# A fused routing-attention and expert kernel: the second pair's keys turned on TensorE in the prologue

## The chip, the cores and the metric

The kernel runs on one core of a Trainium2 chip. The metric is the device time of one execution in microseconds. Three runs of the kernel before gave 945.76, 945.78 and 945.89 us; the median is 945.78. A core has TensorE (PE in the profile; its weight loads are PEld), VectorE (DVE), ScalarE (ACT), GpSimd (POOL) and the DMA queues, of which that of SyncE (SP) issues nearly all loads here.

## The reference

Two blocks are computed one after the other. The first is attention in which a query may look only at keys that were assigned to the same one of 16 centroids:

```
q_assign = argmax(q_n . c_n)          # 4 batches, 8 heads, 768 tokens, 64 values a head
k_assign = argmax(k_n . c_n)          # q_n, k_n, c_n: divided by their lengths
mask     = q_assign[:, None] == k_assign[None, :]
scores   = where(mask, scale * q @ k.T, -1e9)
attn     = softmax(scores, over the keys)
x        = attn @ v
```

The second is `h = x @ w_in`, `g = h * erf(softplus(h))`, `out = g @ w_out` with 3072 tokens, 512 inputs and 2048 inner values. All inputs and the output are float32.

## The kernel before

The 32 combinations of batch and head are worked as 16 pairs of heads. For a pair, `qT` and `kT` hold queries and keys with the 2 x 64 values of the heads on the 128 partitions and the 768 tokens in a row. The function `load` brings queries and keys in by 32 x 32 blocks: four DMAs a tensor, each for one head and half its values, so that one VectorE transpose by blocks of 32 (`transposes`, or `transposed_part` for some columns) makes `qT` or `kT`. Values `v` are loaded token by token in two DMAs. Pair 1's queries and keys use `x_more` as their place, since the ordinary buffers hold pair 0.

For each pair, `similarities` makes the products with the centroids into PSUM bank `turned[1]`, and `choose`, a generator, goes on in steps on VectorE: `sims` (a transpose), a maximum over the centroids, `hot` (which centroid is the maximum), `hotT` (its transpose). It stops behind each step until the code calls `next` or `run`. `masks` multiplies `hotT` by a constant matrix `pick` and copies the product into `qm` or `km`, the rows that add a large number where query and key were assigned alike. `vectors` makes the bfloat16 copies `qv` and `kv`.

`maxima_step` finds the greatest score of each query ahead of the exponentials: a pass of `qv` with `kv` and a pass of `qm` with `km` add up in PSUM (`wide`, or in the prologue `also`, two banks each), and VectorE reduces them into `nmx`. When half of a pair's queries are done, VectorE reduces `nmx` into `lowest`, and `turn` puts the results into a row of `qm` by TensorE and ScalarE. Then come, for each half of the queries and each block of 128 keys (a unit), `products` (scores into `sc`), `scores` (the masks added to them), `curve` (the exponential on ScalarE), `accumulate` (GpSimd) and `attend` (products with `v` into `turned[0]` or `turned[1]`).

The order is written out by hand. Every instruction keeps its program order on its engine. Waits between engines follow from the tiles that instructions read and write.

The prologue runs from the loads to the loop over `period`. It makes pair 0's `qT`, `kT`, similarities, `choose(0)`, three of the four masks, then the five maxima steps of `FIRST_STEPS`, alternating between `also` and `wide`, then `step_ahead(0, 0)`, the next such step, then `turn(0, 0)` and the transposes of pair 1. Between these lie `warm` calls, products on TensorE whose results nobody reads. In `period(0, 0)` the code issues `products`, `step_ahead(0, 1)`, `scores`, `curve`, and then the similarities of pair 1; `period(0, 1)` begins with `step_ahead(0, 2)`, which writes `wide` again. The rest of `choose(1)` is spread over these two periods.

`places` are five staging areas for the weights of the second block; the fifth is a part of `x_more`, and `fetch` of it stands behind the prologue's last transposes on SP's queue.

Of the kernel before, what the change touches and what calls it, by code (L numbers as in the profile page):

```python
# [139 lines left out]
def kernel(  # L140
# [84 lines left out]
    def load(p, nm, src, pl):  # L225
        if p >= NPAIR:
            return
        b, h0 = heads(p)
        if nm == "v":
            t = pl.tile([P, NJ, 2, D], F32, name="in_v")  # L230
            for e in range(2):
                queues[0].dma_start(out=t[:, :, e], in_=src[b, h0 + e].rearrange("(j p) d -> p j d", p=P))
        else:

            if pl is None:
                t = x_more.rearrange("p a k t -> p (a k t)")[:, (nm == "k") * S : (1 + (nm == "k")) * S]
                t = t.rearrange("p (n t) -> p n t", t=Q)
            else:
                t = pl.tile([P, NB, Q], F32, name="in_" + nm)
            for e in range(2):  # L240
                for g in range(D // Q):
                    queues[e if nm == "q" else e * g].dma_start(
                        out=t[e * D + g * Q : e * D + (g + 1) * Q],
                        in_=src[b, h0 + e, :, g * Q : (g + 1) * Q].rearrange("(n t) d -> t n d", t=Q),
                    )
        pairs.setdefault(p, {})[nm] = t
# [143 lines left out]
    def transposed_part(p, nm, lo, hi):  # L390

        st = pairs[p]
        t = st[nm].rearrange("p n t -> p (n t)")
        ve.transpose(out=rows[p % 3][nm][:, lo:hi], in_=t[:, lo:hi])
        if hi == S:
            st[nm + "T"] = rows[p % 3][nm]
            del st[nm]

    def similarities(p, groups=range(4), lo=0, hi=HW):

        if p >= NPAIR:
            return
        st = pairs[p]
        st["psim"] = turned[1][:, 0:HW]
        for g in groups:
            te.matmul(
                st["psim"][2 * C * g : 2 * C * (g + 1), lo:hi], lhsT=ccT[:, p % HP],
                rhs=st["qk"[g // 2] + "T"][:, g % 2 * HW + lo : g % 2 * HW + hi],
                start=True, stop=True,
            )  # L410

    def choose(p, spare=None, aside=False):

        if p >= NPAIR:
            return
        st = pairs[p]
        n = HW // C
        sims = routep.tile([P, HW], F32, name="sims")
        ve.transpose(out=sims, in_=st.pop("psim"))
        yield  # L420
        sim = sims.rearrange("p (g c) -> p g c", c=C)
        mx = (wide[:, 0] if spare is None else spare)[:, 512 - n :]
        ve.reduce_max(out=mx, in_=sim, axis=AX.X)
        yield
        hot = routep.tile([P, HW], BF16, name="hot")
        ve.tensor_tensor(
            out=hot.rearrange("p (g c) -> p g c", c=C), in0=sim,
            in1=mx.unsqueeze(2).to_broadcast([P, n, C]), op=ALU.is_equal,
        )
        yield  # L430
        if aside:
            st["aside"] = routep.tile([P, HW], BF16, name="aside")
            ve.transpose(out=st["aside"][D + Q :], in_=hot[D : D + Q])
            yield
        st["hotT"] = routep.tile([P, HW], BF16, name="hotT")
        ve.transpose(out=st["hotT"], in_=hot)
# [978 lines left out]
    def period(p, i):  # L1415
        u = 2 * NJ * p + 2 * i
        n1, n2 = 2 * p - 1, 2 * p
        early = lambda n: 0 <= n < N_EARLY

        def mask(place):  # L1420
            which = (MASKS if p else FIRST_MASKS).get((i, place))
            if which:
                return masks(p + 1, *which, turned[0 if i in (0, 5) else 1], place == 2)
            return lambda: None

        if u > 0:
            for which in turns if i in (0, 3) else ():
                turn(*which)
                turns.remove(which)
            if i == 3 and not p:  # L1430
                transposes(2, "k")
            if i == 3 and p:
                similarities(p + 2)
                routing[0] = choose(p + 2, turned[0], True)
            step_ahead(p, 2 * i)
            if i == 3 and p:
                next(routing[0], None)
            if i == 2:
                transposes(p + 2, "k" if p else "q")
        mask(0)()  # L1440
        if i == 0 and early(n1 - 1):
            sign(n1 - 1)
        elif i == 3 and early(n1):
            sign(n1)
        if i == 4:
            next(routing[0], None)
        next(part[0], None)
        if i == 0 and p:
            run(routing[0])
            transposes(p + 2, "q")  # L1450
        if u == 2:
            next(routing[0])
            next(routing[0])
        products(u)
        mask(3)()
        products(u + 1)
        mask(1)()
        second = step_ahead(p, 2 * i + 1, True) if u > 0 else iter(())
        next(second, None)
        if u == 0:  # L1460
            step_ahead(0, 1)
        rows = D if u == 0 or u + NJ + 2 >= len(units) else Q
        scores(u, rows)
        next(second, None)
        next(second, None)
        next(part[0], None)
        if i == 5:
            next(routing[0], None)
        scores(u + 1, rows)
        later = mask(2)  # L1470
        if i == 3 and not p:
            similarities(p + 2)
            routing[0] = choose(p + 2, turned[0], True)
        if i == 0:
            later()
            curve(u)
        else:
            curve(u)
            later()
        curve(u + 1)  # L1480
        if u == 0:
            similarities(1)
            routing[0] = choose(1, turned[1])
            next(routing[0])
            vectors(1, "q")
            vectors(1, "k")
        if i == 0 and early(n1 - 1):
            bounded(n1 - 1)
            shifted(n1 - 1)
        elif i == 1 and early(n1):  # L1490
            size_and_rest(n1)
        elif i == 5 and early(n2):
            rest(n2)
        for _ in range(FORMS.get(p, {}).get(i, 0)):
            x_forms.pop(0)() if x_forms else forms.pop(0)[0]()
        if i == 3:
            if not p:
                next(routing[0], None)
            if early(n1):
                bounded(n1)  # L1500
                shifted(n1)
        elif i == 1:
            load(p + 1, "v", v, vp)
            if p == 0:
                run(routing[0])
        elif i == 4:
            vectors(p + 2, "k")
            vectors(p + 2, "q")
        if u > 0:
            if i == 1 and early(n1 - 1):  # L1510
                summed(n1 - 1)
            elif i == 4 and early(n1):
                summed(n1)
            if i in POOL_FORMS.get(p, ()) and forms:
                forms.pop(0)[1]()
            for w in (u - 2, u - 1):
                accumulate(w)
            for w in (u - 2, u - 1):
                attend(w)
            if i == 3:  # L1520
                next(routing[0], None)
            if i % HJ == 0 and u - 1 != LATE or u - 3 == LATE:
                part[0] = divide(u - 1 - u % NJ)
                next(part[0])
        if i == 3 and early(n2):
            size(n2)
# [29 lines left out]
    for r in (0, D):  # L1556
# [8 lines left out]
    products(0)  # L1565
    warm(9, turned[0], zeros)
    run(choose(0))
    copies = [
        masks(0, nm, half, bank)
        for nm, half, bank in (("q", 0, wide[:, 0]), ("k", 0, turned[0]), ("k", 1, turned[1]))  # L1570
    ]
    transposed_part(1, "q", 0, 2 * P)
    ve.tensor_scalar_max(out=st["qm"][:, 0:HW], in0=wide[:, 0, 0:HW], scalar1=0.0)
    transposed_part(1, "q", 2 * P, 5 * P)
    for copy in copies[1:]:
        copy()
    load(0, "v", v, vp)
    for n in range(len(places) - 1):
        fetch(n)
    for i, pieces in enumerate(FIRST_STEPS):  # L1580
        run(maxima_step(0, pieces, wide if i % 2 else also, by_products=True))
        if i == 1:
            masks(0, "q", 1, turned[1])()
        if 0 < i < len(FIRST_STEPS) - 1:
            warm(2, turned[0], zeros)
    step_ahead(0, 0)
    warm(2, turned[0], zeros)
    turn(0, 0)
    transposed_part(1, "q", 5 * P, S)
    turns.clear()  # L1590
    transposes(1, "k")
    fetch(len(places) - 1)
    queues[0] = queues[1] = sy
    for p in range(NPAIR):
# [108 lines left out]
```

## Time and profile before

| what | value |
|---|---|
| profiled execution | 945.83 us |
| its span | 944.1 us |
| PE busy | 938.0 us (99%) |
| DVE busy | 784.3 us (83%) |
| ACT busy | 546.6 us (58%) |
| POOL busy | 506.4 us (54%) |
| TensorE clock granted, first 10 us | 1.00 |

The times in the rows below are microseconds from the start of the span; a row of a timeline gives the start, the length, the engine, the line, the operation, the tiles `out<-in`, the shape and the count, and in brackets how long the engine sat idle before and who ended that. All instructions that a helper records have one line, L131, so the tile names tell them apart; `sc` in the prologue is `also` as well as the score tiles, since they share a pool. A row of the chain is start, length and what set the pace. In a group of instructions the numbers behind the bar are the busy time in us and the mean ns of one. In a table of windows each engine's busy time and count stand in the order PE, PEld, DVE, ACT, POOL, and then the clock granted to TensorE, the share of the DMA engines and GB/s.

### The profile page before, as it was taken

Reading aid. Unit: us, or ns where it says so; the run is one execution under the profiler, and the core shown is the slowest. Engines: PE = TensorE matmul, PEld = TensorE weight load, DVE = VectorE, ACT = ScalarE, POOL = GpSimd, SP = SyncE. Lnnn points to the kernel's source line nnn. Section 1 sums busy time; section 2 is a strip of 40 time slices with the busy share of each in tenths; the row PEclk is TensorE's granted clock in tenths of the full one; section 3 lists DMA queues with packets and bytes.
Section 4 is the critical chain, followed back from the end, with each engine's and each line's share of the span. In section 5 each row is a group of like instructions: output and inputs, shape, how many; then the busy total and the mean of one; then the engine's idle time right before and its main releaser. Section 6 shows DMA issues by size and latency. Waiting matters only on the chain.

```text
span 944.1 us, 22367 instructions
## 1 busy us (share of the span) xinstructions
PE 938.0 (99%) x8775; PEld 708.9 (75%) x8775; DVE 784.3 (83%) x1416; ACT 546.6 (58%) x809; POOL 506.4 (54%) x365
## 2 busy tenths in 40 slices
PE   8999999999999999999999999999999999999998
PEld 4555555555555555688888889998999899989987
DVE  8888888888888887879886688689868977897887
ACT  4777777777777776476413553663257236525541
POOL 2688888888888888999119111450063016103600
PEclk9999999999999999999999999999999999999999
DMA  9345545554443621133875257353453436343433
GB/s 215 79 112 113 113 113 114 113 114 112 113 112 68 156 56 38 24 128 127 219 249 219 83 125 221 106 175 118 151 176 128 136 120 202 118 150 123 157 112 111
DMA packets 176352, 123.17 MB, mean 130 GB/s; under 512 B 132600, under 2 KB 143352, under 8 KB 176248
## 3 DMA queue, kind: packets, MB, share of 16 engines
q1 hardware_dynamic: 171880, 116.34, 43.2%
q0 software_dynamic: 1872, 4.98, 2.9%
q8 instruction: 69, 1.13, 0.5%
q10 hardware_dynamic: 2496, 0.43, 0.2%
q14 instruction: 35, 0.29, 0.1%
HBM read 91.78 MB, written 23.33 MB: 122 GB/s over the span
## 4 chain that ended last, share of the span: by engine, by line
PE 98%; DVE 1%; SPq 0%; DMA 0%; issue 0%; DVEq 0%
PE bank L131 43%; PE turned L131 32%; PE sc L131 17%; PE wide L131 6%; DVE nmx L131 1%; SPq L131 0%; DMA qm<-least_rows 0%; DVE sims L131 0%; DVE hotT L131 0%; DVE wide L131 0%; DVE hot L131 0%; DVE qm L131 0%; DVE qT L131 0%; DVE osb L131 0%; DVEq L1698 0%
## 5 line engine op out<-in xcount | busy, mean ns | idle before, releaser
L131 POOL TENSOR_TENSOR more_out<-more_out,pr 128x768 f32<-128x768 f32 x128 | 217.1, 1696 | 15.4 <-ACT pr L131 5.4
L131 DVE TENSOR_REDUCE nmx<-wide 128x2 f32<-128x512 f32 (+4 forms) x189 | 179.4, 950 | 45.6 <-PE wide L131 44.5
L131 ACT ACTIVATE pr<-sc 128x768 f32<-128x768 f32 x192 | 148.4, 810 | 80.4 <-PE wide L131 73.8
L131 PE MATMUL turned<-pr,in_v 128*32 128x193 f32 x3072 | 145.2, 330 | 0.0
L131 POOL TENSOR_TENSOR g<-g 128x512 f32<-128x512 f32 x36 | 47.1, 1308 | 180.8 <-DVE g L131 178.9
L131 PEld LDWEIGHTS turned<-pr,in_v 128*32 128x32 f32 x3072 | 90.2, 109 | 51.0 <-issue 27.0
L131 DVE TENSOR_TENSOR g<-g 128x512 f32<-128x512 f32 x132 | 90.8, 688 | 23.2 <-PE bank L131 12.2
L131 PE MATMUL sc<-qT,kT 64*128 64x384 f32 x528 | 98.7, 485 | 0.0
L131 DVE TENSOR_TENSOR g<-bank,g 128x256 f32<-128x256 f32 (+1 forms) x128 | 64.6, 531 | 18.2 <-PE bank L131 9.5
L131 PE MATMUL bank<-g_more,g 128*128 128x256 f32 (+1 forms) x328 | 75.7, 374 | 0.0
L131 PE MATMUL bank<-x_own,w_in 128*128 128x128 f32 (+1 forms) x440 | 74.0, 310 | 0.0
L131 ACT ACTIVATE a_s<-g 128x1024 f32<-128x1024 f32 x38 | 39.6, 1055 | 57.5 <-POOL g L131 44.7
L131 POOL TENSOR_TENSOR more_out<-pr,pr 128x768 f32<-128x768 f32 x32 | 59.6, 1861 | 14.9 <-ACT pr L131 14.9
L131 PEld LDWEIGHTS bank<-g_more,g 128*128 128x128 f32 x328 | 61.2, 190 | 8.1
L131 PEld LDWEIGHTS bank<-x_own,w_in 128*128 128x128 f32 x440 | 63.2, 191 | 4.4 <-issue 0.6
L131 DVE TENSOR_TENSOR g<-a_s,g 128x512 f32<-128x512 f32 x76 | 66.2, 892 | 0.4 <-ACT a_s L131 0.4
L131 PE MATMUL wide<-kv,qv 64*128 64x512 bf16 (+4 forms) x380 | 64.4, 326 | 0.5 <-DVE nmx L131 0.5
L131 PE MATMUL bank<-w_out,g 128*128 128x256 f32 x280 | 64.5, 379 | 0.0
L131 PE MATMUL wide<-km,qm 32*128 32x512 bf16 (+5 forms) x380 | 62.0, 325 | 0.0
L131 ACT ACT_TABLE_LOAD x40 | 51.3, 1283 | 17.9 <-DVE g L131 17.3
L131 PEld LDWEIGHTS <-qv 64*128 64x128 bf16 x386 | 23.0, 93 | 51.4 <-issue 37.1
L131 PEld LDWEIGHTS sc<-qT,kT 64*128 64x128 f32 x528 | 46.3, 187 | 18.6 <-issue 1.3
(245 smaller groups left out, 1992.6 us busy)
## 6 DMA issues: line engine op xcount, KB each, us to landing
g_more<-b_dram SPq DMA_DIRECT2D x52, 512.0 KB
g_more<-w_dram SPq DMA_DIRECT2D x84, 256.0 KB
x_own<-in_moe_w_in_dram SPq DMA_DIRECT2D x13, 512.0 KB
in_v<-in_v_dram SPq DMA_DIRECT2D x32, 192.0 KB
x_dram<-more_out SPq DMA_DIRECT2D x128, 48.0 KB
x_own<-x_dram SPq DMA_DIRECT2D x6, 1024.0 KB
in_k<-in_k_dram SPq DMA_DIRECT2D x59, 96.0 KB
in_q<-in_q_dram SPq DMA_DIRECT2D x58, 96.0 KB
```

The lines of the kernel that those rows point to most:

```text
L131: ins = getattr(self.engine, name)(*args, **kw)
```

## The change

Pair 1's keys are loaded token by token, with two DMAs like those of the values, into the same part of `x_more`. Six float32 transposes on TensorE (`turned_by_products`), three behind the second maxima step into `turned[0]` and three behind the third into `turned[1]`, with one ScalarE copy of 384 columns each, make `kT`; the VectorE transpose of the keys and two of the `warm` calls go. Pair 1's queries are turned in two VectorE pieces and not three, both ahead of the maxima.

The similarities of pair 1 stand before `step_ahead(0, 0)`, and the first two steps of `choose(1)` behind it; `hot` moves to `period(0, 0)` and `hotT` to the start of `period(0, 1)`.

The product for the first half of pair 0's query mask is made in two parts: 128 columns into `wide`, copied by VectorE, and 256 columns into `also[:, 0, 256:512]`, copied by ScalarE behind the two key masks.

```diff
@@ load
-        if nm == "v":
-            t = pl.tile([P, NJ, 2, D], F32, name="in_v")
+        if nm == "v" or (nm == "k" and pl is None):
+            if nm == "v":
+                t = pl.tile([P, NJ, 2, D], F32, name="in_v")
+            else:
+                t = x_more.rearrange("p a k t -> p (a k t)")[:, S : 2 * S]
+                t = t.rearrange("p (j e d) -> p j e d", j=NJ, e=2)
             for e in range(2):
                 queues[0].dma_start(out=t[:, :, e], in_=src[b, h0 + e].rearrange("(j p) d -> p j d", p=P))
...
+    def turned_by_products(p, nm, bank, half):
+
+        st = pairs[p]
+        st[nm + "T"] = rows[p % 3][nm]
+        for j in range(HJ):
+            te.transpose(
+                out=bank[:, j * P : (j + 1) * P],
+                in_=st[nm][:, half * HJ + j].rearrange("p e d -> p (e d)"), identity=ident,
+            )
+        ae.copy(out=st[nm + "T"][:, half * HW : (half + 1) * HW], in_=bank[:, 0:HW])
...
@@ period
         if u == 2:
-            next(routing[0])
-            next(routing[0])
+            run(routing[0])
...
         if u == 0:
-            similarities(1)
-            routing[0] = choose(1, turned[1])
             next(routing[0])
             vectors(1, "q")
             vectors(1, "k")
...
         elif i == 1:
             load(p + 1, "v", v, vp)
-            if p == 0:
-                run(routing[0])
...
@@ prologue
-    copies = [
-        masks(0, nm, half, bank)
-        for nm, half, bank in (("q", 0, wide[:, 0]), ("k", 0, turned[0]), ("k", 1, turned[1]))
-    ]
+    first_queries, other_queries = wide[:, 0, 0:P], also[:, 0, 2 * P : 2 * P + HW - P]
+    te.matmul(first_queries, lhsT=pick[0:D, 0], rhs=st["hotT"][0:D, 0:P], start=True, stop=True)
+    te.matmul(other_queries, lhsT=pick[0:D, 0], rhs=st["hotT"][0:D, P:], start=True, stop=True)
+    copies = [masks(0, "k", half, turned[half]) for half in range(2)]
     transposed_part(1, "q", 0, 2 * P)
-    ve.tensor_scalar_max(out=st["qm"][:, 0:HW], in0=wide[:, 0, 0:HW], scalar1=0.0)
-    transposed_part(1, "q", 2 * P, 5 * P)
-    for copy in copies[1:]:
+    ve.tensor_scalar_max(out=st["qm"][:, 0:P], in0=first_queries, scalar1=0.0)
+    transposed_part(1, "q", 2 * P, S)
+    for copy in copies:
         copy()
+    ae.activation(out=st["qm"][:, P:HW], in_=other_queries, func=ACT.Relu)
...
-        if 0 < i < len(FIRST_STEPS) - 1:
+        if i in (1, 2):
+            turned_by_products(1, "k", turned[i - 1], i - 1)
+        elif i == 3:
             warm(2, turned[0], zeros)
+    pairs[1].update(lows[1])
+    del pairs[1]["k"]
+    similarities(1)
     step_ahead(0, 0)
+    routing[0] = choose(1, turned[1])
+    next(routing[0])
+    next(routing[0])
     warm(2, turned[0], zeros)
     turn(0, 0)
-    transposed_part(1, "q", 5 * P, S)
     turns.clear()
-    transposes(1, "k")
```

More of the change, by code (lines that the diff above doesn't have):

```diff
@@ L235, in load @@
             if pl is None:
-                t = x_more.rearrange("p a k t -> p (a k t)")[:, (nm == "k") * S : (1 + (nm == "k")) * S]
+                t = x_more.rearrange("p a k t -> p (a k t)")[:, 0:S]
                 t = t.rearrange("p (n t) -> p n t", t=Q)
```

## The prediction

> **What bounds the kernel now.** I read the page first, then the chain that ended last in order of time, then the start of each engine's timeline, and last the waits and the loads. The page's rows of span, busy time and chain:
>
> ```profile
> span 944.1 us, 22367 instructions
> PE 938.0 (99%) x8775; PEld 708.9 (75%) x8775; DVE 784.3 (83%) x1416; ACT 546.6 (58%) x809; POOL 506.4 (54%) x365
> PE 98%; DVE 1%; SPq 0%; DMA 0%; issue 0%; DVEq 0%
> ```
>
> TensorE carries 98% of the chain, so a shift of TensorE's start of steady work travels to the end one to one, unless a later wait absorbs it. The change lies wholly before the main loop and in its first two periods, so only the first 25 us matter. The chain there:
>
> ```profile
> 10.86 0.32 PE wide L131
> ...
> 11.23 0.55 DVE qm L131
> ...
> 12.26 5.17 DVE nmx L131 x5
> ...
> 17.53 0.19 DVE lowest L131
> ...
> 17.77 0.34 PE turned L131 x6
> ...
> 19.65 0.89 PE turned L131 x8
> ...
> 20.54 0.40 PE wide L131 x4
> 20.94 1.29 PE sc L131 x8
> ```
>
> To be seen: from 11.23 to 17.72 the end is set by VectorE (a mask, a transpose, five maxima, the `lowest` reduction), and from 17.77 on by TensorE alone, where the chain stays for the rest of the stretch. So two moments count: L, when `lowest` starts (17.53), and X, when `step_ahead(0, 2)` starts on TensorE (20.54). Whatever moves X moves the end. VectorE's own rows:
>
> ```profile
> 8.42 0.58 DVE L131 STREAM_TRANSPOSE sims<-turned 128x384 f32<-128x384 f32 x1 [0.62 <-PE turned L131]
> 9.04 0.56 DVE L131 TENSOR_REDUCE wide<-sims 128x24 f32<-128x384 f32 x1
> 9.64 0.55 DVE L131 TENSOR_TENSOR hot<-sims,wide 128x384 bf16<-128x384 f32 x1
> ...
> 10.73 0.40 DVE L131 STREAM_TRANSPOSE qT<-x_more 128x256 f32<-128x256 f32 x1
> 11.21 0.56 DVE L131 TENSOR_SCALAR qm<-wide 128x384 bf16<-128x384 f32 x1
> 11.69 0.57 DVE L131 STREAM_TRANSPOSE qT<-x_more 128x384 f32<-128x384 f32 x1
> 12.20 0.69 DVE L131 TENSOR_REDUCE nmx<-sc 128x2 f32<-128x512 f32 x1
> 12.81 1.22 DVE L131 TENSOR_REDUCE nmx<-wide 128x2 f32<-128x1024 f32 x1
> ...
> 17.62 0.95 DVE L131 TENSOR_REDUCE nmx<-wide 128x2 f32<-128x768 f32 x1
> 18.48 0.30 DVE L131 STREAM_TRANSPOSE qT<-x_more 128x128 f32<-128x128 f32 x1
> 18.71 0.93 DVE L131 STREAM_TRANSPOSE kT<-x_more 128x768 f32<-128x768 f32 x1
> 19.57 0.92 DVE L131 TENSOR_REDUCE nmx<-wide 128x2 f32<-128x768 f32 x1
> ```
>
> X follows the last of these: 19.57 + 0.92 = 20.49, and 0.05 later TensorE may overwrite `wide`. The similarities of pair 1 end at 19.65 + 0.89 = 20.54 too, so X is held twice over; taking one holder away frees nothing.
>
> **The change part by part.**
>
> *The first maxima step: where the new wait is.* Rows of TensorE and ScalarE at that place, and ScalarE's group for a 256-column read of PSUM:
>
> ```profile
> 11.88 0.28 PE L131 MATMUL sc<-km,qm 64*128 64x256 bf16 x2 [0.41 <-ACT km L131]
> 11.99 0.39 PE L131 MATMUL wide<-kv,qv 64*128 64x512 bf16 x2
> ...
> 12.82 0.50 PE L131 MATMUL turned<-lowest,identb 128*128 128x384 bf16 x2
> 13.25 0.39 PE L131 MATMUL sc<-kv,qv 64*128 64x512 bf16 x2
> ```
>
> ```profile
> 11.25 1.05 ACT L131 ACTIVATE km<-turned,nbig 128x384 bf16<-128x384 f32 x2 [2.58 <-PE turned L131]
> ...
> 18.16 0.96 ACT L131 CAST qm<-turned 1x384 bf16<-1x384 f32 x2 [4.74 <-PE turned L131]
> ```
>
> ```profile
> L131 ACT COPY g_more<-turned 128x256 f32<-128x256 f32 x13 | 4.8, 366 | 4.3 <-DVE g_more L131 3.8
> ```
>
> Now the first step's second pass waited 0.41 us for ScalarE's `km`, not for VectorE's `qm`; shortening `qm` from 384 columns to 128 therefore saves VectorE about 0.3 us that nobody waits for. The change puts `other_queries` into columns 256 to 511 of bank 0 of `also`, and the first maxima step writes columns 0 to 255 of that same bank. ScalarE reads `other_queries` only after both `km` copies. Whether TensorE must wait for a reader of other columns of a bank is decided by these rows of period (0, 3):
>
> ```profile
> 31.69 1.49 PE L131 MATMUL turned<-pr,in_v 128*32 128x193 f32 x32
> ...
> 33.25 0.56 DVE L131 TENSOR_REDUCE turned<-sims 128x24 f32<-128x384 f32 x1 [0.41 <-PE turned L131]
> ```
>
> That reduction writes columns 488 to 511 of `turned[0]`; its input was there, yet it idled 0.41 us until the 32 products into columns 0 to 385 of the same bank ended (31.69 + 1.49 = 33.18). Order is kept by bank, not by column. So I take the wait as real. [...]
>
> The working: one more query product precedes the key products; a second product of 384 columns adds some 0.16 to the first (two in 0.50, from the row of 12.82, against one in 0.32 to 0.35), so 128 columns are some 0.05 and `km` starts at 11.30. The two copies take 1.05 less an overlap with the next of about 0.1 (VectorE's 11.21 + 0.56 overlaps 11.69 by 0.08), the read of 256 columns 0.37: 11.30 + 0.94 + 0.37 = 12.61, released at 12.66. The step's first pass takes 0.11 (as 11.88 to 11.99) and from its second pass to VectorE's maximum lie 12.20 - 11.88 = 0.32, so the first maximum starts at 13.09 in place of 12.20: +0.89. Bounds: +0.05 if columns decide, +1.0 if the new product costs 0.15. The value next to the row of 33.25 is +0.89. Behind the waiting instruction on TensorE stand the whole first and second steps; VectorE waits for them with nothing else to do (its remaining query transpose, 512 columns in one piece, ends near 12.0).
>
> *The following maxima.* The rows from 12.81 to 17.43 come from five reductions without a gap, so L moves by the same +0.89, if TensorE keeps up. It must do three transposes after steps 1 and 2 in place of two warm-up products:
>
> ```profile
> 5.82 0.42 PE L131 MATMUL turned<-ident,pr 128*128 128x128 f32 x1
> ...
> 6.03 0.97 PE L131 MATMUL turned<-lowest,identb 128*128 128x384 bf16 x3
> ```
>
> ```profile
> L131 PE MATMUL bank<-x_own,w_in 128*128 128x128 f32 x296 | 38.4, 275 | 0.0
> ```
>
> The one float32 transpose held TensorE 0.21 us (5.82 to 6.03); the same shape as a product takes 38.4 / 296 = 0.13. Three are 0.39 to 0.63, against about 0.33 for two warm-up products of 384 columns (0.16 each). So +0.06 to +0.30 a step. VectorE spends (5.17 - 0.61) / 4 = 1.14 on each later maximum; with the first at 13.09 the second starts at 13.70 and step 2 must be ready at 14.84. It starts at 13.25 + 0.89 + 0.06 to 0.30 = 14.20 to 14.44 and needs about 0.6 (0.22 for a first pass of 512 columns, then the 0.32 and a little for longer rows): ready at 14.80 to 15.04. Cost 0 to 0.2 a step; I take 0, since the row of the same shape is the product's 0.13. What hides it is VectorE's maximum; without that cover it costs 0.12 to 0.60. ScalarE's two copies of 384 columns go into the 4.74 us in which it idles before 18.16 now.
>
> *The similarities before `step_ahead(0, 0)`.* Their 0.89 us leaves TensorE's path after L and goes between step 4 and `step_ahead(0, 0)`, which now waits for `wide`:
>
> ```profile
> 16.34 0.34 PE L131 MATMUL wide<-kv,qv 64*128 64x384 bf16 x2 [0.52 <-DVE nmx L131]
> ```
>
> It is wanted at 17.62 and started at 16.34; 0.89 later less the 0.52 of idling it starts at 16.71 and is ready by 17.25. Cost 0. The gain on TensorE behind L would be 0.89, but X is also held by VectorE, and there nothing gets shorter: out go the rows of 18.48 and 18.71, which delay the row of 19.57 by 1.09; in their place come `sims` and its maximum ahead of that same row, and these two depend on each other, 8.42 to 9.64 = 1.22 where they stood so. That is +0.13. TensorE then idles about 0.9 us ahead of X. `hot` and `hotT` come sooner, and nobody waits for them: their first use is behind X, where TensorE does not stop.
>
> *The loads.*
>
> ```profile
> 6.92 2.35 SPq L131 DMA_DIRECT2D x_more<-in_k_dram  x4
> ...
> 14.11 1.15 SPq L131 DMA_DIRECT2D in_v<-in_v_dram  x2
> ```
>
> ```profile
> 0.00:5.00 5.00, 3.87 (x19) 2.56 (x20) 2.79 (x25) 1.69 (x3) 2.97 (x21) 1.00 0.81 128
> 5.00:10.00 5.00, 5.00 (x31) 2.43 (x30) 3.97 (x8) 1.66 (x2) 1.33 (x8) 1.00 1.06 168
> ```
>
> Four issues of 2.35 become two of the form of 14.11, 1.15: everything behind them on SP goes out 1.2 us sooner, and the last early weight fetch no longer waits for the transpose that ends at 19.64. Nothing on the chain waits for these. The keys must be there by 13.4: the centroids and four blocks of 384 KB are 1.6 MB, the rows move 0.64 + 0.84 = 1.48 MB by 10 us, so they land near 10.7, some 2.7 us early. Cost 0; if they were late, TensorE would stand still with all steps behind it.
>
> *Sum.* +0.89 (bank) + 0.13 (VectorE's order) = +1.02 on X. The profiled execution took 945.83 (span 944.1 and 1.73 around it), 0.05 over the median of 945.78; 945.83 + 1.02 - 0.05 = 946.8.
>
> **The rivals.**
>
> *Columns decide, no bank wait.* For it: the two ranges do not overlap. Against it: the row of 33.25. Then only +0.05 and +0.13 are left: 946.0, to 945.7 if dependent pairs run closer.
>
> *The prologue gets shorter.* Mechanism: TensorE's similarities were the true holder of X and VectorE's order does not bind, so their 0.89 leaves the path: 945.78 - 0.89 = 944.9. It decides only if the maximum of 19.57 ends 0.9 sooner than I find. For it, the similarities end exactly at X; against it, 20.49 + 0.05 is X as well, and the swap on VectorE is even.
>
> *The transposes or their keys come late.* If each transpose is exposed at its full 0.42 in place of 0.13, three cost 1.26 and each of the two steps is late by up to 0.5: 946.8 + 0.4 to 1.0 = 947.2 to 947.8. Against it: the next product started 0.21 after the transpose.
>
> [...]
>
> **How the numbers follow.** Forecast (bank wait, 946.5 to 947.1) 0.64; no bank wait 0.17; shorter prologue 0.06; late transposes or keys 0.08; clock 0.05. 0.2% is 1.9 us, about what a measurement of this kernel tells from no change: 943.9 to 947.7. Faster needs about twice the third case: 0.01. Slower takes in the clock and a third of the late transposes: 0.08. The rest, 0.91, is within. The range leaves out the third case, the clock and the worse half of the late ones: 945.7 to 947.4. The likeliest case lies above the old time, though within the bound.
>
> **What would show it.** In the changed profile the first `sc<-kv,qv` should start near 12.7, with TensorE idle for ScalarE's `qm` (right) or at 11.0 (bank step wrong). The first maximum should start near 13.1 and `lowest` near 18.4; `sims` should follow the first 768-wide maximum at once; TensorE should idle some 0.9 us ahead of the third `wide<-kv,qv` behind `lowest`, which starts near 21.5. [...] The prediction is wrong if X stays at or below 20.5, or if a later DMA or VectorE wait grows or absorbs the shift.

## The result and the profile after

The changed kernel takes 947.10 us (median of 22 runs, 946.71 to 947.83), the kernel before 945.79 (22 runs, 945.63 to 946.16). The ratio is 1.0014, with a 95% interval of 1.0007 to 1.002: slower by 1.3 us, the interval being 0.7 to 1.9 us. The forecast was 946.8, within 0.2% of the time before. The profiled execution of the changed kernel took 947.19 with a span of 945.3, against 945.83 and 944.1.

The page of the changed kernel, its rows of span, TensorE and granted clock:

```profile
span 945.3 us, 22370 instructions
PE 937.9 (99%) x8778; PEld 708.9 (75%) x8778; DVE 783.0 (83%) x1414; ACT 547.9 (58%) x812; POOL 506.9 (54%) x365
PEclk9999999999999999999999999999999999999999
```

TensorE and VectorE do a little less work than before (937.9 and 783.0 us busy against 938.0 and 784.3), and the granted clock of this execution is 1.00, as before. The time is not in anybody's work; it is in a wait. The chain in order of time shows where:

```profile
10.90 0.21 PE wide L131
11.12 0.14 PE turned L131
...
11.29 1.05 ACT km L131 x2
12.34 0.28 ACT qm L131
...
12.66 0.41 PE sc L131 x4
...
13.17 5.23 DVE nmx L131 x5
...
18.49 0.18 DVE lowest L131
18.67 0.86 DVE nmx L131
19.53 0.50 DVE sims L131
...
20.05 0.56 DVE turned L131
20.61 0.87 DVE nmx L131
...
21.52 0.39 PE wide L131 x4
21.92 1.29 PE sc L131 x8
```

Two things are new. Between the query mask and the first maximum the chain now runs through ScalarE: both key masks and then the copy of the other queries. And from `lowest` to the third step behind it the chain stays on VectorE until 21.48, where before it was on TensorE. The rows of TensorE's timeline at both places:

```profile
12.66 0.28 PE L131 MATMUL sc<-kv,qv 64*128 64x256 bf16 x2 [1.25 <-ACT qm L131]
...
13.56 0.55 PE L131 MATMUL turned<-ident,x_more 128*128 128x128 f32 x3
14.04 0.39 PE L131 MATMUL sc<-kv,qv 64*128 64x512 bf16 x2
...
21.52 0.28 PE L131 MATMUL wide<-kv,qv 64*128 64x256 bf16 x2 [0.86 <-DVE nmx L131]
```

In the kernel before, the first of these steps went without a wait:

```profile
11.02 0.27 PE L131 MATMUL sc<-kv,qv 64*128 64x256 bf16 x1
```

ScalarE's rows of the changed kernel, the last of which reads `sc`, that is `also`:

```profile
11.29 1.05 ACT L131 ACTIVATE km<-turned,nbig 128x384 bf16<-128x384 f32 x2 [2.56 <-PE turned L131]
12.23 0.38 ACT L131 ACTIVATE qm<-sc 128x256 bf16<-128x256 f32 x1
```

The first maxima step stands still for 1.25 us until ScalarE's `qm` is done. The `qm` of that copy are the queries 128 to 383, and the step works on queries 0 to 127 and begins with a pass that reads `qv` and `kv` alone, so it is not their data that it waits for. Later TensorE idles 0.86 us, the time that the moved similarities used to fill. VectorE's rows:

```profile
10.27 0.58 DVE L131 STREAM_TRANSPOSE hotT<-hot 128x384 bf16<-128x384 bf16 x1
...
11.36 0.70 DVE L131 STREAM_TRANSPOSE qT<-x_more 128x512 f32<-128x512 f32 x1
13.17 0.69 DVE L131 TENSOR_REDUCE nmx<-sc 128x2 f32<-128x512 f32 x1 [1.10 <-PE sc L131]
...
18.49 0.18 DVE L131 TENSOR_REDUCE lowest<-nmx 128x6 bf16<-128x18 f32 x1
18.58 0.95 DVE L131 TENSOR_REDUCE nmx<-wide 128x2 f32<-128x768 f32 x1
19.45 0.57 DVE L131 STREAM_TRANSPOSE sims<-turned 128x384 f32<-128x384 f32 x1
20.05 0.56 DVE L131 TENSOR_REDUCE turned<-sims 128x24 f32<-128x384 f32 x1
20.52 0.95 DVE L131 TENSOR_REDUCE nmx<-wide 128x2 f32<-128x768 f32 x1
```

The first maximum starts at 13.17, where it started at 12.20; the four that follow have no gap; the two steps of `choose(1)` take the place of the two transposes.

The start of the same `hotT`, which lies ahead of everything that changed, differs between executions (10.03 to 10.27 over all traces below; 10.27 and 10.10 in two of the changed kernel). So positions are compared from there. In the kernel before it is this row:

```profile
10.22 0.58 DVE L131 STREAM_TRANSPOSE hotT<-hot 128x384 bf16<-128x384 bf16 x1
```

L is the start of `lowest`, X that of `step_ahead(0, 2)` on TensorE, both counted from the start of `hotT`. The times before were 945.83, 945.85 and 945.90 beside the three groups of runs of the experiments; each ratio is against its own group's.

| kernel | L | X | X - L | time, us | ratio and its 95% interval |
|---|---|---|---|---|---|
| before | 7.31 | 10.32 | 3.01 | 945.79 | |
| changed | 8.22 | 11.25 | 3.03 | 947.10 | 1.0014 (1.0007 to 1.002) |
| split_alone | 8.22 | 11.24 | 3.02 | 946.55 | 1.0008 (0.9999 to 1.0016) |
| mask_whole | 7.38 | 10.41 | 3.03 | 946.23 | 1.0005 (0.9996 to 1.0014) |
| other_bank | 7.85 | 10.88 | 3.03 | 946.64 | 1.0008 (0.9999 to 1.0017) |
| copy_between | 7.76 | 10.79 | 3.03 | 946.64 | 1.0009 (1.0 to 1.0017) |
| later_product | 7.30 | 10.33 | 3.03 | 945.84 | 1.0 (0.9991 to 1.0009) |
| similarities_back | 7.31 | 10.19 | 2.88 | 946.35 | 1.0006 (0.9997 to 1.0015) |
| max_later | 7.30 | 10.11 | 2.81 | 945.81 | 1.0001 (0.9992 to 1.001) |
| after_again | 8.22 | 11.25 | 3.03 | 947.25 | 1.0014 (1.0004 to 1.0024) |
| mask_whole_again | 7.37 | 10.40 | 3.03 | 946.60 | 1.0008 (0.9998 to 1.0017) |

The intervals are about 0.9 us to either side, as wide as most differences between these kernels, and one kernel, mask_whole, gave 946.23 and then 946.60 with the same X. What decides is therefore the place and size of a wait in the trace; the times are a loose cross-check.

### The profile page after: what moved, and what is told of

The parts are those of the page before. It is cut to its first block, busy times and chain, and to the rows that moved or that the text cites. A ratio compares the mean times of both kernels' runs of the same rounds, so it can differ in the third digit from the quotient of the medians.

```text
span 945.3 us, 22370 instructions
## 1 busy us (share of the span) xinstructions
PE 937.9 (99%) x8778; PEld 708.9 (75%) x8778; DVE 783.0 (83%) x1414; ACT 547.9 (58%) x812; POOL 506.9 (54%) x365
## 4 chain that ended last, share of the span: by engine, by line
PE 98%; DVE 1%; SPq 0%; DMA 0%; ACT 0%; issue 0%; DVEq 0%
PE bank L131 43%; PE turned L131 32%; PE sc L131 17%; PE wide L131 6%; DVE nmx L131 1%; SPq L131 0%; DMA qm<-least_rows 0%; DVE sims L131 0%; ACT km L131 0%; DVE hotT L131 0%; DVE wide L131 0%; DVE hot L131 0%; DVE turned L131 0%; DVE osb L131 0%; ACT qm L131 0%
## 5 line engine op out<-in xcount | busy, mean ns | idle before, releaser
L131 DVE TENSOR_TENSOR g<-bank,g 128x256 f32<-128x256 f32 (+1 forms) x128 | 64.6, 531 | 18.4 <-PE bank L131 9.4
```

Source lines behind the costliest of these rows:

```text
L131: ins = getattr(self.engine, name)(*args, **kw)
```

## The experiments

The theory: the first maxima step is ordered behind ScalarE's read of the other queries because both lie in one PSUM bank, and this makes nearly the whole loss; VectorE's saved work brings nothing because X has two holders. The rivals: the turned keys or the moved similarities cost; ScalarE's additional copy costs wherever it reads; columns and not banks set the order. A third unit is possible too, the whole tile: `also` and `wide` are tiles of two banks each, one for each head. Most of the runs cannot tell the bank from the tile; the rows of other_bank can.

**split_alone: the query mask in two parts, nothing else**, put into the kernel before.

```diff
-    copies = [masks(0, nm, half, bank) for nm, half, bank in (("q", 0, wide[:, 0]), ...)]
+    first_queries, other_queries = wide[:, 0, 0:P], also[:, 0, 2 * P : 2 * P + HW - P]
...
+    ae.activation(out=st["qm"][:, P:HW], in_=other_queries, func=ACT.Relu)
```

> The kernel before with the two-part query mask alone; keys, similarities and `choose(1)` as before. Bank theory: the first maximum starts near 13.15, `lowest` near 18.45, `step_ahead(0, 2)` near 21.45, time 946.7, or 947.0 if the whole measured difference of 1.3 belongs to this part. Rival, the other parts cost: `lowest` later by less than 0.2 and 945.8.

Measured: 946.55, L at 8.22 and X at 11.24 from `hotT`, the same to 0.01 us as in the changed kernel. TensorE's row:

```profile
12.42 0.28 PE L131 MATMUL sc<-kv,qv 64*128 64x256 bf16 x2 [1.25 <-ACT qm L131]
```

The same 1.25 us. This part alone makes the whole shift of X, +0.92 us. The absolute positions lie 0.2 ahead of the expected ones because `hotT` started at 10.03.

**mask_whole: the changed kernel with that part undone.**

```diff
-    first_queries, other_queries = wide[:, 0, 0:P], also[:, 0, 2 * P : 2 * P + HW - P]
...
+    copies = [masks(0, nm, half, bank) for nm, half, bank in (("q", 0, wide[:, 0]), ...)]
...
+    ve.tensor_scalar_max(out=st["qm"][:, 0:HW], in0=wide[:, 0, 0:HW], scalar1=0.0)
```

> The changed kernel with its first query mask made in one product into `wide` and copied whole by VectorE, as before; keys, similarities and order of `choose(1)` stay as changed. Bank theory: TensorE no longer waits for ScalarE ahead of the first maxima step, the first maximum starts near 12.3 in place of 13.17, `lowest` near 17.6 in place of 18.49, `step_ahead(0, 2)` near 20.6 in place of 21.52, and the time falls by about 0.9 to 946.2. Rival, the loss comes from the turned keys or the earlier similarities: `lowest` comes early all the same, but the time stays at 947.1.

Measured: 946.23, L at 7.38 and X at 10.41. The turned keys, their loads, the six transposes and the moved similarities together shift X by no more than 0.09, of which 0.07 lies ahead of L: the query transpose is one piece of 512 columns here, and VectorE reaches the first maximum 2.09 behind `hotT`'s start in place of 1.98. The rival that these parts cost falls for the prologue. The time is 0.4 above the kernel before where X explains 0.1; more on this stands under mask_whole_again.

**other_bank: one address.**

```diff
-    first_queries, other_queries = wide[:, 0, 0:P], also[:, 0, 2 * P : 2 * P + HW - P]
+    first_queries, other_queries = wide[:, 0, 0:P], wide[:, 1, 2 * P : 2 * P + HW - P]
```

> The changed kernel with one address changed: the 256 columns of the other queries go to columns 256 to 511 of bank 1 of `wide`, which the second maxima step writes, in place of bank 0 of `also`, which the first writes. Bank theory: the wait moves to the second step; the first maximum starts near 12.3, TensorE's second step starts at about 12.65 behind ScalarE's copy, the second maximum near 13.35 (13.77 now, 12.81 before), `lowest` near 18.05, time about 946.7. Rival, order by columns: neither step waits, `lowest` near 17.6, 946.2. Rival, the first step needs ScalarE's copy as data: nothing changes, first maximum at 13.2, 947.1.

Measured: 946.64. TensorE's rows, and ScalarE's copy of the other queries:

```profile
11.03 0.27 PE L131 MATMUL sc<-kv,qv 64*128 64x256 bf16 x1
...
11.89 0.28 PE L131 MATMUL sc<-km,qm 64*128 64x256 bf16 x2 [0.41 <-ACT km L131]
12.63 0.39 PE L131 MATMUL wide<-kv,qv 64*128 64x512 bf16 x2 [0.46 <-ACT qm L131]
```

```profile
12.20 0.38 ACT L131 ACTIVATE qm<-wide 128x256 bf16<-128x256 f32 x1
```

The first step no longer waits for ScalarE's `qm`; the second does, since it writes the tile that now holds the other queries. It too works on queries 0 to 127 alone and needs no data of that copy; but its product for head 1 writes columns 0 to 511 of the bank that holds the other queries, so here columns would make that one wait as well. The run decides two things. The first is the first step: without the shared tile it goes at 11.03. The second is the unit. The second step's row of 12.63 is two products, the first for head 0 into bank 0 of `wide` and the next for head 1 into bank 1, where the other queries are. If banks set the order, the first of them would go 0.11 behind the row of 11.89, as in the kernel before (11.88 and 11.99), and only the next would wait. Both stand until 12.63. So in this run order is kept by the whole tile of two banks, not by the bank; the theory's "bank" is to be read as "tile" in the expectations that follow. The second maximum started at 13.35, as expected, and L moved by 0.54.

**copy_between: ScalarE's copy one place sooner.**

```diff
-    for copy in copies:
-        copy()
-    ae.activation(out=st["qm"][:, P:HW], in_=other_queries, func=ACT.Relu)
+    copies[0]()
+    ae.activation(out=st["qm"][:, P:HW], in_=other_queries, func=ACT.Relu)
+    copies[1]()
```

> The changed kernel with ScalarE's copy of the other queries ahead of the second key mask's copy in place of behind it. Bank theory, by size: the copy ends 0.47 us sooner, so the first step starts near 12.2, the first maximum near 12.7, and `lowest` lies some 7.75 us behind the start of `hotT` (8.22 in the changed kernel, 7.31 in the kernel before); time about 946.6. Rival, the wait belongs to the two key copies and not to the other queries' copy: the first step still starts near 12.3, but the second key mask then holds the second step, `lowest` at 8.2 behind `hotT` and 947.0.

Measured: 946.64, and

```profile
11.95 0.28 PE L131 MATMUL sc<-kv,qv 64*128 64x256 bf16 x2 [0.78 <-ACT qm L131]
```

The wait shrinks by 0.47, one key mask's time on ScalarE, and L comes to 7.76, where 7.75 was expected. The wait follows the reader of the tile, in size too.

**later_product: the other queries' product behind the first step, in a free tile (`turned[0]`, of one bank).**

```diff
-    first_queries, other_queries = wide[:, 0, 0:P], also[:, 0, 2 * P : 2 * P + HW - P]
+    first_queries, other_queries = wide[:, 0, 0:P], turned[0][:, 0 : HW - P]
...
     for i, pieces in enumerate(FIRST_STEPS):
         run(maxima_step(0, pieces, wide if i % 2 else also, by_products=True))
+        if i == 0:
+            te.matmul(other_queries, lhsT=pick[0:D, 0], rhs=st["hotT"][0:D, P:], start=True, stop=True)
+            ae.activation(out=st["qm"][:, P:HW], in_=other_queries, func=ACT.Relu)
```

> The changed kernel with the product of the other 256 queries issued behind the first maxima step, into `turned[0]`, whose reader (the first key mask's copy) is done by then, and copied by ScalarE behind both key masks as now. Bank theory: no step waits, first maximum near 12.25, `lowest` near 17.55, `step_ahead(0, 2)` near 20.6, time about 946.2, as with the mask whole. Rival, ScalarE's extra copy is what costs, wherever its source lies: `lowest` stays near 18.5 and the time at 947.1.

Measured: 945.84, L at 7.30, X at 10.33: the kernel before to 0.01 us, with all other parts of the change in place. The same ScalarE copy, from a tile that the step does not write, costs nothing. So ScalarE's work is not the cost, and the other parts neither gain nor lose on the way to X.

**similarities_back: later_product with the similarities and `choose(1)` at their old places.**

```diff
-    similarities(1)
     step_ahead(0, 0)
-    routing[0] = choose(1, turned[1])
-    next(routing[0])
-    next(routing[0])
...
         if u == 0:
+            similarities(1)
+            routing[0] = choose(1, turned[1])
             next(routing[0])
...
```

> The kernel of later_product (no bank wait) with the similarities of pair 1 and all of `choose(1)` back at their places of the kernel before. Theory of two holders: VectorE, now without its two transposes, frees `wide` at about 20.3, but TensorE's similarities, back on the path, end at about 20.55, so `step_ahead(0, 2)` lies 10.3 us behind the start of `hotT` as in both other cases, and the time is 945.8. Rival, the similarities alone held it: with them back the 0.9 us is lost and the time is 946.7; rival, VectorE's transposes alone held it: 945.5.

Measured: X at 10.19, 0.13 sooner than before and not at the 10.3 expected. TensorE's rows:

```profile
19.61 0.52 PE L131 MATMUL turned<-qT,ccT 128*32 128x384 f32 x2
...
20.39 0.28 PE L131 MATMUL wide<-kv,qv 64*128 64x256 bf16 x2
```

Step and similarities follow each other without a wait: with VectorE's two transposes gone, TensorE's similarities are the holder, and they let go 0.13 sooner than VectorE did. In the kernel before VectorE was thus the later of the two holders. Neither rival fits, since X moved neither by 0.9 nor by 0.3. The time, 946.35, does not follow X; see mask_whole_again.

**max_later: later_product with the maximum of `choose(1)` behind that of `step_ahead(0, 1)`.**

```diff
     routing[0] = choose(1, turned[1])
     next(routing[0])
-    next(routing[0])
     warm(2, turned[0], zeros)
...
         if u == 0:
             next(routing[0])
+            next(routing[0])
```

> The kernel of later_product with the maximum of `choose(1)` moved from ahead of the maximum of `step_ahead(0, 1)` to behind it; the similarities stay early. Theory of two holders: now both are gone; the maximum of `step_ahead(0, 1)` starts when its products are ready, near 19.35, and `step_ahead(0, 2)` near 20.3, that is 10.05 us behind the start of `hotT` in place of 10.33; time 945.84 - 0.25 = 945.6, less than both kernels, if by little more than the spread. Rival, a later wait takes the gain back: `step_ahead(0, 2)` comes early but the time stays 945.8.

Measured: 945.81. X is at 10.11, 0.21 sooner than before, close to the 10.05 expected. The gain is not in the time, and the rows of TensorE and its loads say why:

```profile
20.31 0.29 PE L131 MATMUL wide<-kv,qv 64*128 64x256 bf16 x2 [0.64 <-DVE nmx L131]
...
21.11 0.30 PEld L131 LDWEIGHTS sc<-qT,kT 64*128 64x128 f32 x4 [0.37 <-ACT pr L131]
```

The products that follow need the score buffer that ScalarE's second exponential reads, and that ends at 21.06 (19.55 + 1.51) in this kernel and at 21.03 (19.52 + 1.51) before. A third holder: from `hotT`, the `attend` that follows starts at 12.52 (22.72 in the trace) where it started at 12.58 before (22.80), so that less than 0.1 is left of the 0.21. A gain of that size cannot be told from the kernel before by the times.

**after_again and mask_whole_again: where the rest of the loss lies.** Both kernels unchanged.

> The changed kernel once more. If what it loses beyond the prologue (1.31 us by the medians, 0.98 us by the start of `step_ahead(0, 2)`) belongs to the program, the time is again near 947.1; if it belonged to those executions, it is near 946.8.

> The kernel of mask_whole once more. In its trace one exponential of ScalarE starts at 52.12 where it starts at 51.80 in max_later, with everything ahead of it equal to 0.01 us, and TensorE loses the 0.32 us. If that belongs to the program, it is there again and the time is again near 946.2; if it belongs to the execution, the row shifts back and the time comes nearer to 945.9.

Measured: 947.25 and 946.60. The changed kernel came out near 947.1 again, with the same L and X, so its loss beyond X belongs to the program or comes often. mask_whole came out above both of its expected times. Two places behind the prologue show up. The first is ScalarE's exponential near 52 us; first its rows in max_later, then in mask_whole and in mask_whole_again:

```profile
50.66 0.49 ACT L131 ACTIVATE qm<-turned 128x384 bf16<-128x384 f32 x1
51.80 0.81 ACT L131 ACTIVATE pr<-sc 128x768 f32<-128x768 f32 x1 [0.65 <-PE wide L131]
```

```profile
50.66 0.49 ACT L131 ACTIVATE qm<-turned 128x384 bf16<-128x384 f32 x1
...
52.12 0.81 ACT L131 ACTIVATE pr<-sc 128x768 f32<-128x768 f32 x1 [0.97 <-PE turned L131]
```

```profile
52.11 0.81 ACT L131 ACTIVATE pr<-sc 128x768 f32<-128x768 f32 x1 [0.97 <-PE turned L131]
```

With all ahead of it equal to 0.01 us, the same exponential starts 0.32 later, and the exponentials behind it keep the loss to the end of the attention. It was there in both traces of mask_whole and in similarities_back, and in none of the others. It seems to belong to the program, then; what it waits for was not found. The second place is in the expert stage, in the rows of waits and of the chain of after_again:

```profile
PE bank L131 <- ACT osb L131: 0.7, 1, 0.7
```

```profile
587.93 5.31 DMA out_dram<-osb
...
593.34 0.59 ACT osb L131
```

A store of the output still holds the buffer that ScalarE is to fill, and TensorE stands for 0.7 us behind ScalarE. In the changed kernel's first trace (2.2 us in two waits, the longest 1.2) and in the kernel before, ScalarE waits there too, but TensorE does not; the row of the kernel before:

```profile
ACT osb L131 <- DMA out_dram<-osb: 1.1, 1, 1.1
```

mask_whole_again has the same 0.7 and mask_whole does not, so this belongs to the execution. That profiled execution of the changed kernel took 947.89, the longest of its ten runs. copy_between has a smaller one: its chain passes through a store of 4.71 us from 587.39 and ScalarE's `osb` at 592.20, and its distance to the kernel before grows from 0.39 (564.00 against 563.61) to 0.80 (625.27 against 624.47). So part of its time above the kernel before, too, is not the wait in the prologue.

## Why the prediction was right

*The bank wait.* Predicted +0.89 with the first step at 12.66, the first maximum at 13.09 and `lowest` near 18.4. Measured 12.66, 13.17 and 18.49; from `hotT` the shift of L is +0.91. That the first step came at 12.66 to the hundredth is luck: `hotT` started 0.05 later, so the step came 0.05 sooner from there than predicted, and the maximum followed its second pass by 0.40 (12.77 to 13.17) in place of 0.32. ScalarE's two key masks took 0.94 from their start at 11.29 to 12.23, as worked out. The row of 33.25 showed a VectorE write that idled 0.41 us behind TensorE writes of other columns. That a TensorE write behind a ScalarE read is held in the same way was the author's estimate; that row did not show it. It was the decisive step, and the runs bear it out: the first step waited 1.25 us for ScalarE's read of other columns in the changed kernel and in split_alone, 0.78 in copy_between, where that read came one place sooner, and in later_product, where the read is from another tile, X is that of the kernel before (10.33 against 10.32). "Order is kept by bank" names too small a unit, though. The row of 33.25 could not show it, because `turned[0]` is a tile of one bank; in other_bank order went by the tile: the product into one bank of `wide` waited 0.46 us for the read in the other. For this change both give the same wait.

*The following maxima and the transposes.* Predicted cost 0, with three transposes in 0.39 to 0.63. From 13.56 to 14.04 they took 0.48, two warm-up products 0.43 before (12.82 to 13.25). The maxima have no gap.

*VectorE's order.* Predicted +0.13, measured +0.02 (X - L 3.03 against 3.01). This term was mis-sized: the two dependent steps did stand 0.60 apart (19.45 to 20.05), but the maximum of `step_ahead(0, 1)` followed 0.47 behind the second, so the pair delays it by 1.07 and not by 1.22, against 1.09 for the transposes; the maximum itself then took 0.95 where it took 0.92. The step that failed was taking the spacing behind it from the first `choose`, whose next operation depended on it too.

*Two holders of X.* Predicted: nothing gained by the similarities' 0.89 and VectorE's 1.09. Right: TensorE idles 0.86 ahead of X where 0.9 was written, and later_product leaves X where it was. Not quite right is that the two holders end together, so that taking either away frees nothing: similarities_back takes VectorE's away and gains 0.13. `hotT` of pair 1 does come 1.4 sooner, 22.57 against 23.96, and nobody uses it sooner.

*The loads.* Predicted cost 0. The keys cost nothing in the trace: the row of the transposes at 13.56 has no idle time before it, so they did not wait for a DMA.

*The sum.* X was to come at 21.56 and came at 21.52: +0.98 in place of +1.02, of which +0.05 is the later `hotT` and no part of the change. That the two sums lie so close is partly luck, since the +0.11 too much on VectorE's order is made up by the 0.02 too little on the bank wait and by `hotT`. The time came 0.3 above the forecast, inside the range: 947.10 - 945.79 = 1.31 where X gives 0.98. What lies behind the prologue was taken as carried one to one. The shift was 0.95 to 440 us and 1.06 from 457 on in the first trace; the second lost 0.7 at the output store. The step that left this out is the first one, that no later wait changes the shift. Where the rest of the 1.31 arises in the first trace is open.

*The rivals.* Order by columns is excluded by the 1.25 us wait, since the columns do not overlap and no data is shared, together with later_product, in which the same copy from another tile costs nothing. A shorter prologue did not occur. The keys were not late. The clock: the chances give a lowered clock 0.05 and count it in the 0.08 for slower, and no run shows one. The granted clock is 0.999 or 1.00 in every execution of these kernels, and these windows of the changed kernel, with TensorE's longest wait (1.25 us), show 1.00.

```profile
10.00:12.00 2.00, 1.35 (x10) 0.53 (x8) 1.97 (x5) 0.71 (x2) 0.00 (x0) 1.00 1.15 193
12.00:14.00 2.00, 1.34 (x12) 0.73 (x11) 0.90 (x3) 0.94 (x3) 0.00 (x0) 1.00 1.06 169
```

The page's row of clock shows no dip either: it is 9, that is 90% or more, in all 40 slices.

## What to carry to other kernels

In these runs a TensorE write into a PSUM tile waited for ScalarE's read of other columns of that tile (1.25 us in the changed kernel, 0.78 in copy_between) and, in other_bank, of its other bank (0.46 us). So put a piece of work into such a tile only if whoever reads it is done before the next writer of any part of the tile; here a copy of 256 columns that nobody needed yet held up a whole stage for 0.9 us. Before work is taken off a path, list everything that releases its end: X had a holder on VectorE and one on TensorE, and behind them one on ScalarE. Taking TensorE's 0.89 us away brought nothing, taking VectorE's away moved X by 0.13, both together by 0.21, and of that ScalarE left less than 0.1. And a pair of steps should be costed with the operation that follows it, not by its own durations.

## What was not expected

One exponential near 52 us starts 0.32 us later in two of these programs and not in the others, with equal work ahead of it; the cause is open. And a shift of a tenth of a percent in the prologue can meet, or miss, a wait on an output store 570 us later that is worth another 0.7 us: the changed kernel's runs spread over 1.1 us, those of the kernel before over 0.5. That the spread comes from that store is likely from three traces with it (after_again, mask_whole_again and, smaller, copy_between), and was not tried: max_later's runs spread over 1.1 us as well, and its one trace, of an execution of 945.78, shows no such wait.
